# A gated attention and GLU kernel: raw gate and up pieces loaded seven steps ahead, the first round's transposed pieces in other buffers, output weight and last maxima fetched sooner, last sums later

## The chip, the core and the metric

The kernel runs on one core of a Trainium2 chip. The metric is the device time of one execution in microseconds (us), the median of several runs. The core has a matrix engine (PE, with its weight loads shown apart as PEld), a vector engine (DVE), a scalar engine (ACT), GpSimd (POOL), and SyncE (SP), which here does nothing but issue DMA transfers, one after the other in program order. All transfers of this kernel go through SP's one queue, and 16 DMA engines carry them out.

## The reference

The input x has 2048 tokens of 512 features. Two branches are computed from it and mixed with a gate of one number per token:

```python
g = sigmoid((x * gate_w).sum(-1, keepdims=True))
a = attention(x, wqkv, wo)     # 32 heads of 16, causal, window of 256 keys
b = (sigmoid(x @ w_gate) * (x @ w_up)) @ w_down     # hidden width 1376
return g * a + (1 - g) * b
```

All is float32. The kernel multiplies each pair of operands as high and low parts, with three matrix products (high by high, high by low, low by high).

## The kernel before, in words

**Two stretches.** The first stretch is a loop over `u` from 0 to `N - 1` (L764; `N` is 140). In it the attention is computed head group by head group: in step `u` scores by query block with their maxima (`s_part`, for `u` below 128), transposed scores with the exponential nine steps later (`st_part`), and, in every even step, the products with V of two blocks (`pv_part`, L807). Matrix products of the other branch fill the gaps: 72 groups of gate and up (`gu`, nine pieces of 128 hidden features, two matrices, four token chunks of 512), then 16 groups of the tail (`tp`, the last 224 hidden features, computed token block by token block). Results are stored to scratch tensors in DRAM: `gu_scratch`, `tail_scratch`, `oT_scratch` (attention output), `sum_scratch` (softmax sums).

The second stretch is a loop over `n` (L916), 44 steps of `(c, f)`: four rounds `c` of 512 tokens, with eleven pieces `f` of the hidden width each. Step `n` multiplies piece `f` with the down weight into four accumulators (`pd`, lines L79 to L81). At the end of a round the attention output is multiplied with the output weight (`pa`) and the two are mixed and stored.

**Raw pieces.** `h_load(n)` (L672) reads the gate and the up piece of step `n`, 512 KB, from `gu_scratch` into slot `n % 8` of `hv`, which lies over the buffer of V (16 blocks of 560 columns; a slot has 1024). Block by block V is read for the last time in the last steps of the first stretch, the last two blocks at `u` = 138. `h_skew(n)` (L708) prepares later steps: it splits the piece of step `n + 2` into high and low parts (`hb`: ACT L75, DVE L76) and computes sigmoid and product of step `n + 3` (ACT L727, DVE L728). `AHEAD` (L53) says how far ahead the pieces are loaded: `h_load(n + AHEAD)` in step `n` (L918), and the first `AHEAD` of them in the first stretch, every second `u` from `HLOAD = N - 2 * AHEAD` on (L858).

**Transposed pieces.** The pieces `f` = 9 and 10 come from the tail. `tail_read` (L696) reads them from `tail_scratch`, 14 transfers of 64 KB a round, transposed 32 by 32, to the place that `tail_home` (L679) gives: columns of `xh` and `xl` (the high and low parts of x) whose matrix work is done. For round 0 the transfers start at `u = TREAD` (L854), and what is left of them goes out in the first four steps of the second stretch (L921).

**Other transfers around the change.** `max_store` (L342) and `max_load` (L347) take the row maxima of four query blocks through DRAM into the operand `ring` that `st_part` reads; number 31, the last, holds query blocks 12 to 15 of the last group, and `st_part` needs the first of them at `u` = 131. `WO` (L793) loads the output weight, 1 MB, into the buffer that the gate and up weights leave. `sums_load`, `sums_invert` (L735, L739) read the softmax sums of a round, invert them on DVE (L741), and store them back (`rec_scratch`); round 3's are needed from the 34th step on. Transfers that wait for a result of the current step are put in the list `later` and issued with the next step (L781), and after the loop behind each of the last two tail groups (L868).

**What sets the order.** The program order on every engine is written out by hand (`manual_schedule`); an engine takes its instructions in that order, and SP too: a transfer whose wait isn't over holds all behind it.

Of the kernel before, what the change touches and what calls it, by code (L numbers as in the profile page):

```python
# [7 lines left out]
F32 = mybir.dt.float32  # L8
# [15 lines left out]
NC = T // CH  # L24
# [20 lines left out]
SHIFT = 6  # L45
TURN = ((0, 2, 1), (1, 0, 2))
TAIL = 109
TREAD = 136
WD_LOAD = {119: 0, 120: 1, 122: 2, 123: 3, 127: 4, 128: 5, 130: 6, 131: 7, 133: 8, 134: 9, 135: 10}
WO = 128  # L50
WO_SPLIT = {132: 0, 133: 1, 134: 2, 135: 3}
WD_SPLIT = {136: 8, 137: 9, 138: 10}
AHEAD = 5  # L53


@with_exitstack
def gated_mix_kernel(
# [46 lines left out]
    NSTEP = NG * NC  # L104
    NP = NSTEP // 2
    NU = NG * NB
# [3 lines left out]
    def load_d(f):  # L110
        tag = "draw" if f == 10 else "wqraw"
        raw_d[f] = cpool.tile([P, D], F32, tag=tag, name=f"wdraw{f}", bufs=2)
        nc.sync.dma_start(raw_d[f][0:FCH[f]], wd[f * P:f * P + FCH[f], :])
        if f == NF - 1:
            nc.sync.dma_start(raw_d[f][FCH[f]:], wd[f * P:f * P + QB, :])
# [13 lines left out]
    with ExitStack() as actx:  # L129
# [157 lines left out]
        def run_dmas(dmas):  # L287
            for dst, src in dmas:
                nc.sync.dma_start(dst, src)
# [54 lines left out]
        def max_load(s):  # L344
            st = ring[s // 2 % RING].bitcast(F32).rearrange("(a r) j f -> r a j f", r=QB)
            o = s % 2 * CH
            nc.sync.dma_start(  # L347
                st[0, :, 0:2, o:o + CH], max_d[s].rearrange("(p s) l b t -> (s l) p (b t)", p=2),
            )
# [31 lines left out]
        later = []  # L381
# [273 lines left out]
        def slot(h, d, c):  # L655
            return (xh, xl)[h][:, d, c * CH:(c + 1) * CH]
# [21 lines left out]

        def tail_home(c, f, w):  # L679
            k = 2 * (f - NFM) + w  # L680
            h, d, cc = (0, k, 2) if c % 2 == 0 else (1, k + 2, 2) if k < 2 else (0, k, 3)
            return (xh, xl)[h][:, d, cc * CH:(cc + 1) * CH].bitcast(F32)

# [12 lines left out]
        def tail_read(c, n):  # L696
            run_dmas(treads[c][:n])
            del treads[c][:n]
# [33 lines left out]
        def flat(v, c):  # L732
            return v[c].rearrange("h (q t) -> (h q) t", t=P)

        def sums_load(c):  # L735
            sm[c] = cpool.tile([P, P], F32, tag="sm", name=f"sm{c}", bufs=2)
            nc.sync.dma_start(sm[c], flat(sum_d, c))

        def sums_invert(c):  # L739
            t = sm.pop(c)  # L740
            nc.vector.reciprocal(t, t)  # L741
            return flat(rec_d, c), t
# [8 lines left out]
        N = NU + PVLAG + 1  # L751
        SUMS = NU - 13 + PVLAG + 1
        U_LAST = 4 * (NSTEP - 2 - 5)
        HLOAD = N - 2 * AHEAD
        done = 0
# [8 lines left out]
        for u in range(N):  # L764
            if u == LAG:
                vctx.close()
                ppool = actx.enter_context(tc.tile_pool(name="ppool", bufs=1))
                pv = ps.tile([P, CH], F32, tag="pv", name="pv", bufs=1)
                behind.append(lambda: nc.vector.memset(pv, 0.0))
            if u == 1:  # L770
                proj_post(NC)
            if u == 4:
                load_gu(0, 0)
                load_gu(0, 1)
            if u % 8 == 1 and u > 8 and u // 8 + 1 < NP:
                sdma = stack_build(u // 8 + 1)
            if u % 16 == 8 and u // 16 + 2 < NG:
                raw_q = load_wqk(u // 16 + 2)
            if u % 4 == 0 and 0 < u <= NU:
                max_store(u // 4 - 1)  # L780
            run_dmas(later)  # L781
            later.clear()
            run_dmas(sdma[:SD])
            del sdma[:SD]
            if u % 4 == 1 and 1 < u <= NU + 1:
                max_load(u // 4 - 1)
            if u in WD_LOAD:
                load_d(WD_LOAD[u])
            if u == TAIL:
                tail_room()  # L790
            if TAIL <= u < TAIL + 2 * ND and (u - TAIL) % 2 == 0:
                tail_load((u - TAIL) // 2)
            if u == WO:  # L793
                both = apool.tile([P, ND, CH], F32, tag="w0", name="woraw")
                wo_raw.extend(both[:, d] for d in range(ND))
                nc.sync.dma_start(both, wo.rearrange("(c p) n -> p c n", p=P))
            for s4 in proj_at.get(u, ()):
                if u < LAG:
                    first.insert(0, (
                        lambda k, h, s4=s4: proj_slot(s4, k, h), lambda s4=s4: proj_sum(s4)))  # L800
                else:
                    work.append(proj_group(s4))
            if u == NU + PVLAG - 1:
                hold_group(*rest.pop(0))
            for hh in range(HG):
                if hh == 0 and u % 2 == 0:
                    for w in (u - PVLAG - 1, u - PVLAG):  # L807
                        if 0 <= w < NU:
                            pv_part(w)
                if u < NU:  # L810
                    s_part(u, hh)
                if 0 <= u - LAG < NU:
                    st_part(u - LAG, hh ^ 1 if u < NU else hh)
                if u < LAG:
                    flush(behind)
                    if hh % 2 == 1:
                        upto = n_first * (2 * u + 1 + hh // 2) // (2 * LAG)
                        run_first(upto - done)
                        done = upto
                else:  # L820
                    if behind:
                        behind.pop(0)()
                    if acts and (u < NU or hh % 2 == 1):
                        acts.pop(0)()
                if u >= LAG and (hh < HG - 1 or u % 2 == 0 if u < NU else hh % 2 == 1):
                    next(slots, None)
                    if u >= NU and not (hh == HG - 1 and u % 2 == 1 and u > NU + 1):
                        next(slots, None)
            if u < LAG:
                flush(soon)  # L830
            if u == LAG - 1:
                split_gu(0, 0)
                split_gu(0, 1)
            if u % 4 == 3 and u < NU:
                max_split(u // 4)
            if u // 16 + 2 < NG:
                if u % 16 == 13:
                    acts.append(lambda g=u // 16 + 2, r=raw_q: (
                        split_wqk(g, r, 0), behind.append(lambda: split_wqk(g, r, 1))))
            if 0 <= u - LAG < NU:  # L840
                mask_p(u - LAG)
            if TAIL + 2 <= u <= TAIL + 2 * ND and (u - TAIL) % 2 == 0:
                acts.append(lambda d=(u - TAIL) // 2 - 1: tail_split(d))
            if WD_LOAD.get(u - 1, 8) < 8:
                acts.append(lambda f=WD_LOAD[u - 1]: split_d(f, True))
            if u in WO_SPLIT:
                acts.extend(lambda d=d: wo_split(d) for d in range(WO_SPLIT[u], WO_SPLIT[u] + 1))
            if u in WD_SPLIT:
                acts.append(lambda f=WD_SPLIT[u]: split_d(f, True))
            if SUMS <= u and (u - SUMS) % 4 == 0:  # L850
                sums_load((u - SUMS) // 4)
            if SUMS + 2 <= u and (u - SUMS) % 4 == 2:
                behind.append(lambda c=(u - SUMS) // 4: later.append(sums_invert(c)))
            if u == TREAD:  # L854
                tail_reads(0)
            if u >= TREAD:
                tail_read(0, 3)
            if u >= HLOAD and (u - HLOAD) % 2 == 0:  # L858
                h_load((u - HLOAD) // 2)
            if u >= N - 2:  # L860
                flush(acts)
                flush(behind)
                h_skew(u - N - 1)
        h_skew(-1)
        spare = [ppool.tile([P, 3, CH], F32, tag="pt", name=f"spare{k}", bufs=3) for k in range(3)]
        for group in rest:
            hold_group(*group)
            run_dmas(later)  # L868
            later.clear()
        assert not (work or first or going or behind or acts or raw_gu or sdma or pts or obs)  # L870

        def blocks(v):
# [13 lines left out]
        def gate():  # L886
            nc.scalar.activation(gs, gsum, AF.Sigmoid)
            nc.vector.tensor_scalar(omg, gs, -1.0, 1.0, op0=ALU.mult, op1=ALU.add)
# [27 lines left out]
        for n, (c, f) in enumerate(steps):  # L916
            if n + AHEAD < len(steps):
                h_load(n + AHEAD)  # L918
            h_skew(n)
# [11 lines left out]
                ]  # L931
            if n == 2:
                gate()
                last_sums = sums_invert(NC - 1)
            if n == 3:
                nc.sync.dma_start(*last_sums)
            if f < 8 and f % 2 == 0 and n > 0 or n == 1:
                o_load(4 * c + f // 2)
# [82 lines left out]
```

## Time and profile before

| what | us |
|---|---|
| median of 3 runs (lowest, highest) | 740.25 (738.74, 741.25) |
| the profiled execution, its own time | 739.3 |
| its span in the profile | 737.6 |
| first score maxima to last (`u` below 128), to about | 531 |
| rest of the first stretch, to about | 568.8 |
| round 0 of the second stretch, to about | 599.7 |
| round 1; round 2 | 40.9; 40.9 |
| round 3 with the last stores | 56.1 |

The chain of work that ended last runs over PE for 95% of the span, over DMA for 2% and over DVE for 2%. The largest groups of DMA transfers are 72 stores of 256 KB to `gu_scratch` and 36 loads of 512 KB from it.

How to read it: times in a timeline are us from the start of the span; a row gives start, length, engine, source line, operation, what it writes and reads, and in brackets the engine's idle time before it with what ended it. "SPq" is SP's queue: such a row is the issuing of a transfer, not the transfer. A matmul's row starts when PE starts it, and matmuls overlap, so the step from one start to the next is the pace. In the rows by stretch each engine has its busy us, then the number of its instructions; the last three columns are the granted clock of PE (1.00 is full), the mean busy share of the 16 DMA engines (their packets overlap a little, so it can pass 1) and GB/s.

### The profile page before, as it was taken

The numbers are of one execution on the slowest core, as the hardware profiler recorded it, in microseconds if no ns is written. First come the engines' busy times: TensorE is split into PE (matmuls) and PEld (weight loads), VectorE is DVE, ScalarE is ACT, GpSimd is POOL, SyncE is SP. The second block draws the span as 40 slices with busy tenths as digits, with TensorE's granted clock in tenths as the row PEclk, the third lists the DMA queues.
The fourth block names the chain that finished last, engine by engine and source line by source line (L and its number), as shares of the span: only waits on it lengthen the run. The fifth ranks groups of instructions, "written<-read, shape, count | busy, mean of one in ns | idle before, by whom it ended". The sixth has DMA issues, their size and how long they took to land.

```text
span 737.6 us, 17720 instructions
## 1 busy us (share of the span) xinstructions
PE 731.2 (99%) x6298; PEld 578.4 (78%) x6298; DVE 507.6 (69%) x1519; ACT 431.4 (58%) x922; POOL 170.6 (23%) x256
## 2 busy tenths in 40 slices
PE   9999999999999999999999999999999999999997
PEld 7888777887777878778777777777877778887886
DVE  5378867667776776776777677677846685848473
ACT  6423676576666666757657667675666573535341
POOL 5200333233232233323223322332341000000000
PEclk9999999999999999999999999999999999999999
DMA  8441334534435353452543525545287878879551
GB/s 295 111 116 44 101 103 123 154 82 131 131 113 142 89 149 113 124 150 68 156 114 103 152 72 138 157 128 152 68 261 215 231 196 201 194 182 228 143 133 57
DMA packets 94464, 103.65 MB, mean 141 GB/s; under 512 B 44942, under 2 KB 57486, under 8 KB 94376
## 3 DMA queue, kind: packets, MB, share of 16 engines
q1 hardware_dynamic: 94376, 102.53, 50.8%
q8 instruction: 49, 0.80, 0.5%
q14 instruction: 39, 0.32, 0.1%
HBM read 45.32 MB, written 31.99 MB: 105 GB/s over the span
## 4 chain that ended last, share of the span: by engine, by line
PE 95%; DMA 2%; DVE 2%; issue 1%; SPq 0%; ACT 0%; DVEq 0%; ACTq 0%
PE gu L245 28%; PE pv L394 12%; PE pj L245 11%; PE s L315 7%; PE st L361 5%; PE tp L539 5%; PE pd L81 4%; PE pd L79 4%; PE pd L80 4%; PE vh L576 3%; PE pa L79 2%; PE pa L81 2%; PE pa L80 2%; DMA V<-gu_scratch 1%; PE vps L440 1%; DVE junk L321 1%
## 5 line engine op out<-in xcount | busy, mean ns | idle before, releaser
L321 DVE CUSTOM_DVE_ANT_0 junk<-s,mask 128x384 f32<-128x384 f32 (+2 forms) x512 | 271.3, 530 | 123.6 <-PE s L315 56.2
L366 ACT ACTIVATE pt<-st 128x384 f32<-128x384 f32 (+2 forms) x512 | 240.9, 474 | 166.7 <-PE st L361 63.3
L245 PE MATMUL gu<-xh,w 64*128 64x512 f32 x1152 | 271.2, 393 | 0.0
L245 PE MATMUL gu<-xl,w 64*128 64x512 f32 x576 | 183.1, 392 | 0.0
L371 POOL TENSOR_SCALAR_AFFINE_SELECT pt<-pt 128x512 f32<-128x512 f32 x128 | 86.4, 675 | 373.7 <-ACT pt L366 370.1
L361 PE MATMUL st<-ring 64*128 64x384 f32 (+2 forms) x536 | 168.2, 332 | 0.1
L315 PE MATMUL s<-ring 64*128 64x384 f32 (+2 forms) x536 | 166.9, 329 | 0.7 <-DVE mx L321 0.7
L245 PEld LDWEIGHTS gu<-xh,w 64*128 64x128 f32 x1152 | 151.2, 185 | 13.6
L315 PEld LDWEIGHTS s<-ring 64*128 64x128 f32 x536 | 95.4, 184 | 39.9 <-DVE nm L332 8.1
L361 PEld LDWEIGHTS st<-ring 64*128 64x128 f32 x536 | 96.4, 184 | 10.5 <-issue 2.7
L394 PE MATMUL pv<-pt,V 128*32 128x384 f32 (+2 forms) x1408 | 91.0, 389 | 0.0
L245 PEld LDWEIGHTS gu<-xl,w 64*128 64x128 f32 x576 | 87.8, 185 | 3.9
L245 PE MATMUL pj<-xl,wqh 64*128 64x512 f32 (+1 forms) x228 | 80.1, 392 | 0.0
L245 PE MATMUL pj<-xh,wqh 64*128 64x512 f32 (+1 forms) x228 | 79.8, 392 | 0.0
L376 POOL TENSOR_SCALAR_AFFINE_SELECT pt<-pt 128x512 f32<-128x512 f32 x112 | 74.7, 667 | 0.0
L245 PE MATMUL pj<-xh,wql 64*128 64x512 f32 (+1 forms) x228 | 69.9, 391 | 0.0
L394 PEld LDWEIGHTS pv<-pt,V 128*32 128x32 f32 x1408 | 37.2, 109 | 35.0 <-issue 28.8
L79 PE MATMUL pd<-ring,hb 128*128 128x512 f32 x160 | 63.2, 395 | 0.3 <-ACT hb L75 0.3
L81 PE MATMUL pd<-ring,hb 128*128 128x512 f32 x160 | 63.1, 394 | 0.1
L80 PE MATMUL pd<-ring,hb 128*128 128x512 f32 x160 | 62.2, 389 | 0.0
L75 ACT CAST hb<-V 128x512 fp32r<-128x512 f32 x40 | 24.9, 622 | 52.5 <-DVE V L728 50.0
L245 PEld LDWEIGHTS pj<-xh,wql 64*128 64x128 f32 (+1 forms) x228 | 41.2, 185 | 3.1
(129 smaller groups left out, 1132.7 us busy)
## 6 DMA issues: line engine op xcount, KB each, us to landing
gu_scratch<-sp SPq DMA_DIRECT2D x72, 256.0 KB
V<-gu_scratch SPq DMA_DIRECT2D x36, 512.0 KB
ring<-sh SPq DMA_DIRECT2D x128, 128.0 KB
ring<-sl SPq DMA_DIRECT2D x64, 128.0 KB
guraw<-in_wgu_dram SPq DMA_DIRECT2D x18, 256.0 KB
oT_scratch<-ob SPq DMA_DIRECT2D x128, 32.0 KB
xl<-oT_scratch SPq DMA_DIRECT2D x16, 256.0 KB
out_dram<-spare SPq DMA_DIRECT2D x16, 256.0 KB
```

Source lines behind the costliest of these rows:

```text
L79: mm(ps, lh, rh, start=first, stop=False)
L80: mm(ps, lh, rl, start=False, stop=False)
L81: mm(ps, ll, rh, start=False, stop=last)
L245: mm(pt, (wl if w == 2 else wh)[r, d], (xl if w == 1 else xh)[r, d, c * CH:(c + 1) * CH], start=k == 0 and not second, stop=k == 3 * ND - ...
L315: mm(pt[:, (k - k0) * P:(e - k0) * P], lhsT, blk(g, k, hh, 1, e - k), start=k == k0, stop=e == i + 1, skip_group_check=True,)
L321: nc.vector.tensor_tensor_reduce(junk[:, 0:n], pt[:, 0:n], mask[:, 3 * P - n:], scale=1.0, scalar=NEG, op0=ALU.add, op1=ALU.max, accum_out ...
L361: mm(pt[:, (q - j) * P:(e - j) * P], lhsT, blk(g, q, hh, 0, e - q), start=q == j, stop=e == last, skip_group_check=True,)
L366: nc.scalar.activation(pts[u][:, hh, 0:n], pt[:, 0:n], AF.Exp, scale=SCALE)
L371: nc.gpsimd.affine_select(p[:, :, 0:P], p[:, :, 0:P], pattern=[[0, HG], [1, P]], compare_op=ALU.is_ge, fill=0.0, base=0, channel_multiplie ...
L376: nc.gpsimd.affine_select(p[:, :, 2 * P:], p[:, :, 2 * P:], pattern=[[0, HG], [-1, P]], compare_op=ALU.is_gt, fill=0.0, base=0, channel_mu ...
L394: mm(pv[32 * hh:32 * hh + 32, (q % 4) * P:(q % 4 + e - q) * P], V[:, j, h * VW:h * VW + 32], p[:, hh, (q - j) * P:(e - j) * P], start=Fals ...
L539: mm(tp[b][:, 0:TW], (xl if w == 1 else xh)[r, d, b * P:(b + 1) * P], tw[d][int(w == 2)][r, 0:TW], start=k == 0 and not second, stop=k == ...
```

## The change

Six edits:

- `AHEAD` from 5 to 7. Seven pieces are loaded in the first stretch, from `u` = 126 in place of 130, and in step `n` piece `n + 7`.
- The transposed pieces of round 0 go to columns 512 to 1023 of `xh` and `xl` for `d` 2 and 3, in place of columns 1024 to 1535 of `xh`. The tail groups read the new place in token blocks 4 to 7, the old one in 8 to 11.
- They are read from `u` = 133, two a step, in place of 136, three a step. Seven steps of two make all 14 in the first stretch; four steps of three left two.
- The output weight is loaded at `u` = 125 in place of 128.
- The last maxima are loaded at `u` = 128, right behind their store and one down weight, in place of 129.
- The sums of round 3 are loaded at step 3 of the second stretch, inverted at step 6 and stored at step 7, in place of the last `u`, step 2 and step 3. What the two last tail groups store goes out at step 3 as well.

```diff
-TREAD = 136
+TREAD = 133
-WO = 128
+WO = 125
-AHEAD = 5
+AHEAD = 7
...
         def tail_home(c, f, w):
             k = 2 * (f - NFM) + w
+            if c == 0:
+                return slot(k // 2, 2 + k % 2, 1).bitcast(F32)
...
-            if u % 4 == 1 and 1 < u <= NU + 1:
+            if u % 4 == 1 and 1 < u < NU:
                 max_load(u // 4 - 1)
             if u in WD_LOAD:
                 load_d(WD_LOAD[u])
+            if u == NU:
+                max_load(NSTEP - 1)
...
-            if SUMS <= u and (u - SUMS) % 4 == 0:
+            if SUMS <= u < N - 1 and (u - SUMS) % 4 == 0:
                 sums_load((u - SUMS) // 4)
...
             if u >= TREAD:
-                tail_read(0, 3)
+                tail_read(0, 2)
...
         for group in rest:
             hold_group(*group)
-            run_dmas(later)
-            later.clear()
...
             if n == 2:
                 gate()
+            if n == 3:
+                run_dmas(later)
+                sums_load(NC - 1)
+            if n == 6:
                 last_sums = sums_invert(NC - 1)
-            if n == 3:
+            if n == 7:
                 nc.sync.dma_start(*last_sums)
```

## The prediction

> **What bounds the kernel now.** I read the page first, then the rows by stretch, then the chain of waits, and last the timelines of SP and PE around the places that these named. The page:
>
> ```profile
> PE 731.2 (99%) x6298; PEld 578.4 (78%) x6298; DVE 507.6 (69%) x1519; ACT 431.4 (58%) x922; POOL 170.6 (23%) x256
> ```
>
> PE is busy for 731.2 of the span's 737.6 us, and the change neither adds nor takes a matmul. So all that it can move is PE's standing time, 6.4 us by this row, and small standstills between matmuls that the row still counts as busy. The rows by stretch say where the 6.4 us lie (time, then PE's busy us; the granted clock is 1.00 in all of them):
>
> ```profile
> 0.00:20.00 20.00, 18.47 (x78) 14.85 (x79) 9.88 (x16) 12.45 (x21) 12.04 (x14) 1.00 0.83 289
> ...
> 531.00:568.80 37.80, 37.69 (x370) 30.64 (x362) 19.97 (x44) 24.21 (x57) 12.60 (x18) 1.00 0.74 220
> 568.80:599.70 30.90, 30.59 (x133) 23.73 (x132) 23.84 (x45) 18.18 (x32) 0.00 (x0) 1.00 0.84 234
> 599.70:640.60 40.90, 40.90 (x185) 33.18 (x184) 27.48 (x49) 18.75 (x33) 0.00 (x0) 1.00 0.80 193
> ...
> 722.30:737.60 15.30, 11.56 (x53) 9.08 (x52) 3.69 (x5) 2.42 (x4) 0.00 (x0) 1.00 0.18 69
> ```
>
> The start (1.53 us) and the end (3.74 us) are out of the change's reach: it touches nothing before `u` = 125 and nothing behind step 34. In its reach lie 531 to 568.8 and round 0, with 0.11 and 0.31 us, and in round 1 PE never stands, though pieces are loaded only five steps ahead there too. The chain of waits names a transfer at one place of round 0 that matters:
>
> ```profile
> 576.15 5.06 DMA V<-gu_scratch
> ...
> 582.68 0.85 DVE sm L741
> ```
>
> A raw piece issued at 576.15 lands 5.06 us later; sigmoid, gate and the inversion of the last sums follow, and then PE. Here the change can gain, and it is small.
>
> **The change part by part. First, the raw pieces (AHEAD, and the sums with them).** SP's timeline shows why that piece, number 5, was late, and PE's what it cost:
>
> ```profile
> 573.23 0.33 SPq L737 DMA_DIRECT2D sm<-sum_scratch  x1
> 573.61 1.49 SPq L289 DMA_DIRECT2D xh<-tail_scratch  x3
> 575.20 0.91 SPq L289 DMA_DIRECT2D tail_scratch<-tt  x2
> 576.15 0.46 SPq L675 DMA_DIRECT2D V<-gu_scratch  x1
> ```
>
> ```profile
> 582.48 0.39 PE L80 MATMUL pd<-ring,hb 128*128 128x512 f32 x1
> 582.70 0.40 PE L81 MATMUL pd<-ring,hb 128*128 128x512 f32 x1
> 583.36 0.50 PE L79 MATMUL pd<-ring,hb 128*128 128x512 f32 x1 [0.26 <-ACT hb L75]
> 583.70 0.39 PE L80 MATMUL pd<-ring,hb 128*128 128x512 f32 x1
> 584.13 0.50 PE L81 MATMUL pd<-ring,hb 128*128 128x512 f32 x1
> 584.47 0.39 PE L79 MATMUL pd<-ring,hb 128*128 128x512 f32 x1
> ...
> 586.78 0.39 PE L80 MATMUL pd<-ring,hb 128*128 128x512 f32 x1
> 587.06 0.50 PE L81 MATMUL pd<-ring,hb 128*128 128x512 f32 x1
> 587.40 0.40 PE L79 MATMUL pd<-ring,hb 128*128 128x512 f32 x1
> ```
>
> Ahead of piece 5 on SP stand the load of the last sums, three transposed reads, and the stores of the last two tail groups, which wait for DVE. Matmuls of 512 columns start 0.22 to 0.23 us apart. From 582.70 to 584.47 there are four steps, 1.77 us in place of 4 x 0.23 = 0.92: **0.85 us** lost. At 587.06 the low part is again just in time: 0.62 us for two steps, **0.16 us** lost. The idle time in the row (0.26) shows less than a third of the first, since a late start also costs the matmuls behind it.
>
> After the change pieces 0 to 6 are issued in `u` = 126 to 138, each two steps behind the last reading of the V blocks that it overwrites (piece 0: blocks 0 and 1, read at 124; piece 6: blocks 10 to 12, read at 136), so SP doesn't stand for them. Piece 5 leaves at `u` = 136, where piece 3 left before:
>
> ```profile
> 560.79 0.49 SPq L675 DMA_DIRECT2D V<-gu_scratch  x1
> ```
>
> ```profile
> ACT V L727 <- DMA V<-gu_scratch: 21.0, 15, 4.0
> ```
>
> That is 15 us sooner than 576.15. Its sigmoid then follows ACT's chain instead of the transfer (the second row is ACT's waits for raw pieces, 15 in all; the longest, 4.0 us, is this one), so the split parts of step 5 are ready some 4 us sooner where 0.85 us were wanting. I take the whole 0.85 + 0.16 = 1.01 us as gained; least is 0, if another wait takes its place. The later rounds gain nothing by it: ACT's other waits there cost PE no time. What is late next shows in DVE's rows around step 0, with a transfer of SP's that will matter below:
>
> ```profile
> 558.17 0.37 SPq L737 DMA_DIRECT2D sm<-sum_scratch  x1
> ```
>
> ```profile
> 563.77 0.93 DVE L741 RECIPROCAL sm<-sm 128x128 f32<-128x128 f32 x1
> ...
> 567.41 0.69 DVE L728 TENSOR_TENSOR V<-V 128x512 f32<-128x512 f32 x1 [1.18 <-ACT V L727]
> ```
>
> DVE has two such instructions of 0.69 us a step for the pieces, product and low part, against PE's twelve matmuls of 0.23, 2.8 us: with the pieces there it draws ahead.
>
> The inversion of the last sums goes from step 2 to 6, one instruction of 0.93 us either way. Where it goes DVE is busy for 4.78 of 5.00 us:
>
> ```profile
> 590.00:595.00 5.00, 5.00 (x24) 4.10 (x23) 4.78 (x9) 4.51 (x9) 0.00 (x0) 1.00 0.62 177
> ```
>
> I cost it at nothing, covered by the lead of some 4 us; without that cover it is 0.93 us. In step `n` SP now waits for the slot of step `n - 1` in place of `n - 3`, whose reader (`h_skew(n - 3)`) is ahead of PE; the output loads queue behind it, and DVE needs those three steps later: nothing, unless SP falls behind.
>
> **Second, the last maxima and the output weight.** SP around `u` = 128, PE at `u` = 131, and PE's wait there:
>
> ```profile
> 534.27 0.43 SPq L796 DMA_DIRECT2D woraw<-in_wo_dram  x1
> ...
> 535.90 0.57 SPq L347 DMA_DIRECT2D ring<-max_scratch  x1
> ```
>
> ```profile
> 540.20 0.37 PE L539 MATMUL tp<-tail_hb,xh 64*128 64x450 f32 x1
> 540.41 0.39 PE L361 MATMUL st<-ring 64*128 64x384 f32 x2
> 540.59 0.36 PE L539 MATMUL tp<-tail_hb,xh 64*128 64x450 f32 x1
> ...
> 541.66 0.37 PE L539 MATMUL tp<-tail_wql,xh 64*128 64x450 f32 x1
> 542.14 0.45 PE L361 MATMUL st<-ring 64*128 64x384 f32 x2
> 542.38 0.36 PE L539 MATMUL tp<-tail_wqh,xh 64*128 64x450 f32 x1
> ```
>
> ```profile
> L361 PEldq EVENT_SEMAPHORE  x1: 51/51/51, 542.0 to 542.0; - x1
> ```
>
> The 16 KB of maxima leave at 535.90, behind the 1 MB of the output weight; PE's queue has a wait of its own at 542.0, in the first `st` that needs them, and goes on from there. That is 6.1 us for 16 KB. In the undisturbed round 540.20 to 540.59 takes 0.39 us, the disturbed one 541.66 to 542.38 takes 0.72: **0.33 us** lost. After the change the weight leaves in `u` = 125, behind the maxima before, where the queue is nearly empty:
>
> ```profile
> 523.00:530.00 7.00, 7.00 (x92) 6.11 (x82) 6.00 (x23) 3.90 (x9) 2.44 (x4) 1.00 0.19 57
> ```
>
> Its buffer is free: the last `gu` matmul starts at 509.17.
>
> ```profile
> 509.17 0.39 PE L245 MATMUL gu<-xh,w 64*128 64x512 f32 x1
> ```
>
> The maxima can leave no sooner than their store has landed, so at about the same time; SP stands there from 534.27 on, 1.6 us at most, with a raw piece and two tail stores behind it: the piece is needed in the second stretch, the stores' buffers four tail groups later. Only 256 KB is ahead of them now. I take 0.33 us as gained; least 0.
>
> **Third, the transposed reads.** 14 reads of 64 KB in 128-byte pieces, the same as before, two a step from `u` = 133 in place of three from 136. Their places are free when the tail groups 4 to 7 are done; the eighth of the 16 stores is the first here:
>
> ```profile
> 546.64 0.38 SPq L289 DMA_DIRECT2D tail_scratch<-tt  x1
> ```
>
> The price of one, from the packets of the 4.2 us from 561.8 on, in which five are issued:
>
> ```profile
> DMA packets 2429, 1.01 MB, mean 241 GB/s; under 512 B 2049, under 2 KB 2172, under 8 KB 2428
> ```
>
> 2049 small packets at 512 a read are four reads, so at most 4.2 / 4 = 1.05 us each. That matters for the third rival. I cost them at nothing: PE needs them in step 9 only. The tail stores put off to step 3 are read in round 3, so nothing again.
>
> **Sum:** 0.85 + 0.16 + 0.33 = 1.34 us less. Against the profiled execution's own 739.3: 738.0. That execution is 0.95 under the median of 740.25; taken off the median it is **738.9 us**. About 0.3% (2.2 us) is what a measurement of this kernel can tell from no change, so this lies within.
>
> **The rivals.** *More than the sum.* The three runs before lie 2.5 us apart, and both stalls hang on when a transfer lands; if a slower run is one in which they are longer, all runs after gather at the fast end. The fastest run less the sum: 738.74 - 1.34 = 737.4. For it: the maxima and piece 5 are the only late transfers behind which PE stood. Against it: the start, which waits for transfers too (DMA 0.83 busy), can vary as much.
>
> *Nothing.* Something else holds step 5: ACT and DVE come out of the first stretch with no lead (the product of step 0 starts only at 567.41), and DVE's two transposes of the last tail groups stay in the way. Then 740.25 less 0.33, 739.9. Against it: ACT's 4.0 us of standing for piece 5.
>
> *The crowd, slower.* From `u` = 132 to 135 four transposed reads go out with two raw pieces; before, it was two raw pieces alone. The loads of sums 2 and of the last down weights queue behind, the sums at 558.17. From 563.77 on DVE stands for late sums, with the low parts of the last weights and the product of step 0 behind it; the 1.18 us of idle time before that product cover the first of that. Four reads at 1.05 us make 4.2 us, less 1.18 is 3.0 us that step 0 starts later: 740.25 - 1.34 + 3.0 = 741.9. It decides when the sums land later than 564.95. For it: the maxima took 6.1 us behind 1 MB, more than the 5.6 from 558.17 to 563.77. Against it: the output weight is gone from the queue by then, and the price is an upper bound. [...]
>
> **How the numbers follow.** The forecast 0.54, within 0.3%. More than the sum 0.2: 737.4 is below 738.0, so faster. Nothing 0.1, the same. The crowd 0.16, of which 0.06 for a time over 742.5, with several such waits. A little of the forecast's own spread falls below 738.0: faster 0.22, same 0.72, slower 0.06. The range goes from 737.4 (the first rival) to 741.0, inside the crowd's 741.9, which leaves out less than 2 in 10.
>
> **What would show it.** In the changed kernel's trace: no step over 0.3 us between `pd` matmuls in steps 1 to 10; the `st` at `u` = 131 0.2 us behind the matmul before it; ACT L727 standing for raw pieces far less than 21.0 us; the reciprocal of sums 2 without idle time before it. Wrong would be a new wait of PE between 550 and 570, or a step 0 that starts later than 568.8.

## The result, and the profile after

| | before, us | after, us | ratio, 95% interval |
|---|---|---|---|
| median of 11 runs each on one chip (lowest, highest) | 740.9 (738.74, 743.55) | 737.95 (737.53, 738.54) | 0.9959 (0.9944 to 0.9974) |
| the profiled execution, its own time | 739.3 | 737.77 | |
| its span | 737.6 | 736.1 | |

The changed kernel is faster by 0.41%; the medians lie 2.95 us apart. (A ratio is worked out from all runs, so it can differ a little from the quotient of the medians.) The forecast of 738.9 was 0.95 us too high. The time lies between it and the 737.4 of the rival *more than the sum*, and what that rival says of the runs came: those after lie 1.0 us apart where those before lay 4.8. (One disturbed run of 1831.75 us of a kernel below is left out of its comparison.)

The page of the changed kernel, its span and busy times:

```profile
span 736.1 us, 17727 instructions
...
PE 730.0 (99%) x6298; PEld 578.3 (79%) x6298; DVE 507.1 (69%) x1519; ACT 430.4 (58%) x922; POOL 170.7 (23%) x256
```

PE stands for 6.1 us in place of 6.4, a difference of 0.3, though the span fell by 1.5: most of what a late start costs is counted as busy. So the starts have to be compared. Three matmuls of each profile, by the timelines of PE (the last `gu` of the first stretch of before, 509.17, and the first `pd`, 568.81, are known); the first `pa` matmul of round 0 in before:

```profile
600.08 0.50 PE L79 MATMUL pa<-xh 128*128 128x512 f32 x1
```

and the last `gu`, the first `pd` and the first `pa` in the changed kernel:

```profile
508.85 0.39 PE L245 MATMUL gu<-xh,w 64*128 64x512 f32 x1
...
568.19 0.48 PE L79 MATMUL pd<-ring,hb 128*128 128x512 f32 x1
...
598.39 0.50 PE L79 MATMUL pa<-xh 128*128 128x512 f32 x1
```

Up to 508.85 the gain is 0.32 us, which the change doesn't reach. From there to the first `pd` it is 59.64 - 59.34 = 0.30 us. Round 0, from the first `pd` to the first `pa`, takes 30.20 in place of 31.27: 1.07 us. The rest loses 0.2. PE's waits in the changed kernel hold only two groups, which before has with the same times, both ahead of the change's reach:

```profile
PE warm_ps L185 <- DVE warm L180: 1.2, 1, 1.2
PE s L315 <- DVE mx L321: 0.7, 2, 0.4
```

At `u` = 131 and in step 5, the two places of the prediction, PE now runs at its pace (timeline of PE in the changed kernel):

```profile
541.31 0.37 PE L539 MATMUL tp<-tail_hb,xh 64*128 64x450 f32 x1
541.36 0.37 PE L539 MATMUL tp<-tail_wql,xh 64*128 64x450 f32 x1
541.52 0.38 PE L361 MATMUL st<-ring 64*128 64x384 f32 x2
541.70 0.36 PE L539 MATMUL tp<-tail_wqh,xh 64*128 64x450 f32 x1
...
582.07 0.39 PE L81 MATMUL pd<-ring,hb 128*128 128x512 f32 x1
582.30 0.39 PE L79 MATMUL pd<-ring,hb 128*128 128x512 f32 x1
582.53 0.39 PE L80 MATMUL pd<-ring,hb 128*128 128x512 f32 x1
582.76 0.39 PE L81 MATMUL pd<-ring,hb 128*128 128x512 f32 x1
```

The `st` starts 0.16 us behind the matmul before it, and between steps 1 and 10 no `pd` start is more than 0.24 behind the last, but for one of 0.32 at the end of step 10, where before has 0.33. SP's order in the changed kernel (timeline of SP):

```profile
562.31 1.97 SPq L675 DMA_DIRECT2D V<-gu_scratch  x1
...
571.64 0.50 SPq L289 DMA_DIRECT2D sum_scratch<-ob  x1
572.50 0.90 SPq L289 DMA_DIRECT2D xl<-tail_scratch  x2
...
577.01 0.86 SPq L289 DMA_DIRECT2D tail_scratch<-tt  x2
578.29 0.32 SPq L739 DMA_DIRECT2D sm<-sum_scratch  x1
```

Piece 5 leaves at 562.31 in place of 576.15, and behind the store of the last sums (571.64) SP goes on 0.36 us after it is issued; the two tail stores and the load of the last sums follow later. In before SP stood there (its waits from 565 to 580 us: the load of the last sums waits for their store):

```profile
SPq L737 <- DMA sum_scratch<-ob: 1.4, 1, 1.4
```

ACT's list of waits has no raw piece any more (21.0 us before).

### The profile page after: what moved, and what is told of

It is laid out like the page before. It is cut to its first block, busy times and chain, and to the rows that moved or that the text cites. A ratio compares the mean times of both kernels' runs of the same rounds, so it can differ in the third digit from the quotient of the medians.

```text
span 736.1 us, 17727 instructions
## 1 busy us (share of the span) xinstructions
PE 730.0 (99%) x6298; PEld 578.3 (79%) x6298; DVE 507.1 (69%) x1519; ACT 430.4 (58%) x922; POOL 170.7 (23%) x256
## 4 chain that ended last, share of the span: by engine, by line
PE 97%; DVE 1%; DMA 1%; issue 1%; ACT 0%; SPq 0%; DVEq 0%
PE gu L245 28%; PE pv L394 12%; PE pj L245 11%; PE s L315 7%; PE st L361 5%; PE tp L539 5%; PE pd L79 5%; PE pd L81 5%; PE pd L80 5%; PE vh L576 3%; PE pa L79 2%; PE pa L80 2%; PE pa L81 2%; PE vps L440 1%; DVE junk L321 1%; DMA V<-in_wv_dram 1%
```

## The experiments

Two theories stood at first: **A**, that transfers which land late at varying times made the runs of before vary, and that AHEAD removes this; **B**, that something else varies. The results brought others in: **C**, the reads make the gain; **D**, the crowd of transfers from 560 to 586; **E**, a standstill of PE is followed by a lower clock; **F** and **G**, the last sums, their store and the last tail stores hold piece 5 up on SP; **H**, the inversion on DVE. Medians stand beside those of the kernel before, run in turn on the same chip.

**The kernel before again**, unchanged, one execution.

> The kernel before, unchanged, for a second profile beside its time. Its runs lie between 738.7 and 743.6 us, those of the changed kernel between 737.5 and 738.5. Theory A (the late transfers vary): where this run is slower than 739.3, the time over it stands in PE's rows at the `st` matmul of u = 131 and in the first steps of the second stretch, and the first 20 us are as before (PE busy 18.5 of 20). Theory B (something else varies, the start or the steady part): those two places lose 0.3 and 1.0 us again, and the excess lies elsewhere.

738.42 us, faster than 739.3, so this execution can't decide between A and B. Piece 5 was late as before (round 0 takes 31.22 us); at `u` = 131 PE's starts show 0.1 us lost (0.48 where 0.38 is the pace) in place of 0.33. So the loss at `u` = 131 varies from run to run, the one in step 5 was there again.

**AHEAD alone.**

```diff
-AHEAD = 5
+AHEAD = 7
```

> Only AHEAD from 5 to 7. Theory A: piece 5 leaves in the first stretch, step 5 of the second stretch has no standstill, profile about 1.0 us under 737.6, and most of the gain of the median too: 738.2 to 739.2, with runs closer together than before's 4.8 us. Theory B: 1.0 us less than before in the median (739.9), runs as far apart as before's. Theory C (the transposed reads' earlier start made the gain): no gain, 740 to 741, since twelve of the reads still go out from u = 136 on, now beside raw pieces.

740.28 (739.12 to 743.16, 12 runs) beside 740.03, ratio 1.0002 (0.9989 to 1.0015): nothing. Its profile, of an execution of 741.26, shows why (timelines of SP, DVE and PE):

```profile
575.03 0.33 SPq L737 DMA_DIRECT2D sm<-sum_scratch  x1
575.41 1.49 SPq L289 DMA_DIRECT2D xh<-tail_scratch  x3
577.00 0.91 SPq L289 DMA_DIRECT2D tail_scratch<-tt  x2
...
580.80 0.65 SPq L893 DMA_DIRECT2D xh<-rec_scratch  x1
...
586.83 0.01 DVE L900 LOAD_MASK_SELECT spare<-xh  x1 [5.25 <-DMA xh<-rec_scratch]
...
588.97 0.50 PE L81 MATMUL pd<-ring,hb 128*128 128x512 f32 x1 [1.71 <-DVE hb L76]
```

Pieces 5 and 6 had left at 561.74 and 568.79. But SP stood as before ahead of the load of the sums, and the reciprocal rows for the attention output (`rec_scratch`) left late behind it: DVE stood 5.25 us for them, and PE 1.71 for DVE. These rows were late in before too (timelines of SP and DVE in before):

```profile
578.96 0.65 SPq L893 DMA_DIRECT2D xh<-rec_scratch  x1
...
584.94 0.01 DVE L900 LOAD_MASK_SELECT spare<-xh  x1
```

They left 10.2 us behind the first `pd` there, 11.0 here, and 6.9 in the changed kernel (575.05). In before DVE, held by piece 5, came to them only at 584.94 and found them landed. So a second wait lay hidden behind the first, one step on and on another engine; moving piece 5 alone laid it open.

PE's waits in this kernel have another new line:

```profile
PE st L361 <- DMA ring<-max_scratch: 0.8, 1, 0.8
```

The weight left at 534.22, a raw piece at 534.75, the maxima at 536.49: with seven pieces one of them stands ahead of the maxima too. PE's wait at `u` = 131 is 0.8 us, and by the starts 1.1 us are lost (541.90 to 543.37 in place of 0.39).

**Maxima and weight alone.** `WO` 125, the last `max_load` at `u == NU`; nothing else.

```diff
-WO = 128
+WO = 125
```

> Only the output weight at u = 125 and the last maxima at u = 128. Theory A: the 0.33 us at u = 131 go, and more in slower runs, so 0.3 to 1.0 us less than before in the median; step 5 keeps its standstill. Theory B: 0.3 us less, which the runs can hardly tell. Theory C: no difference, within 0.3 us.

739.41 (738.38 to 743.74, 12 runs), ratio 0.9995 (0.998 to 1.0011). No loss at `u` = 131, and PE's 0.64 us of idle time in step 5 stays. The term is too small to be told from no change alone.

**The changed kernel with AHEAD 5.**

```diff
-AHEAD = 7
+AHEAD = 5
```

> The changed kernel with AHEAD back to 5, the other edits kept: the transposed reads from u = 133 in their new places, the last sums, maxima and weight as changed. Theory A: piece 5 leaves in step 0, but no longer behind transposed reads, sums and tail stores, so its standstill shrinks or goes; 738.0 to 739.5. Theory B: as the changed kernel but for the 1.0 us of step 5: 738.9. Theory C: the whole gain stays, 737.9 to 738.2.

737.69 (737.35 to 738.08, nine runs), ratio 0.9961 (0.9946 to 0.9976): as fast as the changed kernel. AHEAD is neither enough nor needed. A's attribution falls; its account of the varying stands.

**The reads alone**, sooner and in their new place.

```diff
-TREAD = 136
+TREAD = 133
-                tail_read(0, 3)
+                tail_read(0, 2)
+            if c == 0:
+                return slot(k // 2, 2 + k % 2, 1).bitcast(F32)
```

> Only the transposed reads: from u = 133, two a step, to the new places; five raw pieces ahead, sums, maxima and weight as before. Theory D (the crowd: from 560 to 586 us transposed reads, sums, tail stores, raw pieces and output loads share one queue, and what lands last stops ACT or DVE): the reads are the part that moves most work away, so most of the gain, 738.2 to 739.0, with at most the 0.3 us at u = 131 left over. Theory F (the last sums and the two tail stores ahead of piece 5 are what holds it): step 5 keeps its standstill, 739.5 to 740.2, as far apart as before.

739.23 (738.26 to 741.51, 12 runs) beside 739.65, ratio 0.9995 (0.9982 to 1.0009): nothing, so C falls, and D in so far as it put most of the gain on the reads. Piece 5 left at 577.07, with no reads of round 0 left to pass. PE stood longer than in before, and its clock stayed full (its timeline of PE, then its rows by stretch):

```profile
584.93 0.50 PE L79 MATMUL pd<-ring,hb 128*128 128x512 f32 x1 [2.08 <-ACT hb L75]
```

```profile
584.00:586.00 2.00, 1.02 (x3) 0.59 (x4) 2.00 (x5) 1.15 (x2) 0.00 (x0) 1.00 1.10 345
586.00:588.00 2.00, 2.00 (x10) 1.62 (x10) 1.97 (x5) 1.47 (x3) 0.00 (x0) 1.00 0.72 246
```

**The sums alone**, with the tail stores.

```diff
-            if SUMS <= u and (u - SUMS) % 4 == 0:
+            if SUMS <= u < N - 1 and (u - SUMS) % 4 == 0:
...
-            run_dmas(later)
-            later.clear()
...
+            if n == 3:
+                run_dmas(later)
+                sums_load(NC - 1)
+            if n == 6:
                 last_sums = sums_invert(NC - 1)
-            if n == 3:
+            if n == 7:
                 nc.sync.dma_start(*last_sums)
```

> Only the last sums and the stores of the last two tail groups put off to steps 3, 6 and 7. Theory D: piece 5 leaves a few us sooner but lands behind the same reads, a gain of 0 to 1 us, 739.0 to 740.0. Theory F: most of the gain, 738.0 to 738.6.

738.05 (737.5 to 738.38, 12 runs), ratio 0.9973 (0.9963 to 0.9984): nearly the whole gain, with AHEAD at 5. Its timelines of SP and ACT:

```profile
570.50 0.50 SPq L289 DMA_DIRECT2D sum_scratch<-ob  x1
571.33 1.44 SPq L289 DMA_DIRECT2D xh<-tail_scratch  x3
572.82 0.49 SPq L675 DMA_DIRECT2D V<-gu_scratch  x1
...
577.02 0.63 ACT L727 ACTIVATE V<-V 128x512 f32<-128x512 f32 x1 [0.28 <-DMA V<-gu_scratch]
```

Piece 5 leaves 3.3 us sooner than in before, and ACT stands 0.28 us for it in place of 4.04.

**Reads and sums together** (the two diffs above).

> Both of these edits, neither the seven pieces ahead nor the sooner maxima and weight. Theory D: no standstill of PE over 0.1 us between steps 1 and 10; the whole gain but for the wait at u = 131, 738.0 to 738.5. Theory F: the same as the sums alone.

737.85 (737.5 to 739.04, 12 runs), ratio 0.997 (0.9958 to 0.9981). The reads add nothing that can be measured.

**The kernel before with AHEAD 4**, to make the standstill longer.

```diff
-AHEAD = 5
+AHEAD = 4
```

> The kernel before with AHEAD = 4: piece 4 leaves in step 0, behind sums, reads and tail stores. Theory E (a standstill of some us in the second stretch lowers the granted clock for a while, which makes the slower runs of before: those over 741.3 show a mean clock of 0.997 in place of 1.0): PE stands 2 to 4 us at step 4, the granted clock drops behind it, mean 0.997, and the median is 741 to 744. Without theory E: the same standstill at a clock of 1.0, so only its own length, 740.5 to 742.5. If the number of pieces ahead doesn't matter as long as the crowd is there: as before, 740.

744.77 (744.75 to 748.41, 4 runs), ratio 1.0075 (1.0049 to 1.01). PE stood 2.32 us in step 4. Its rows by stretch, the last three columns clock, DMA and GB/s:

```profile
582.00:584.00 2.00, 1.46 (x5) 0.93 (x6) 1.16 (x2) 1.23 (x3) 0.00 (x0) 0.99 1.02 346
584.00:586.00 2.00, 2.00 (x7) 1.53 (x6) 1.77 (x5) 1.25 (x2) 0.00 (x0) 0.50 1.08 339
586.00:588.00 2.00, 2.00 (x8) 1.60 (x7) 1.97 (x5) 1.08 (x2) 0.00 (x0) 0.66 0.71 241
588.00:590.00 2.00, 2.00 (x10) 1.65 (x9) 1.82 (x4) 1.95 (x5) 0.00 (x0) 1.00 0.61 200
```

Behind the standstill PE got half the clock for (2 x 0.50 + 2 x 0.34) / 0.5 = 3.4 us, 1.7 us lost again. The standstill and the lower clock are what E expects; the median lies above its 741 to 744, since the later rounds lost time as well: in the profile round 1 is 0.55 us longer than in before, and round 3, with a second standstill of 0.96 us and matmuls that start 0.23 us apart again from 718.13 on, 1.6 us.

**Only the two tail stores later**, ahead of the store of the last inverted sums in step 3.

```diff
-            run_dmas(later)
-            later.clear()
...
             if n == 3:
+                run_dmas(later)
                 nc.sync.dma_start(*last_sums)
```

> The kernel before; only the stores of the last two tail groups are put off, to step 3. Theory G (what holds the queue is SP's order: SP stands for the sum store to land before it loads the last sums, then for DVE before the two tail stores, with piece 5 and all else behind): piece 5 leaves about 1 us sooner, a third of the gain, 739.0 to 739.5, runs still 2 to 4 us apart. Theory H (the inversion of the last sums in step 2 on DVE is what costs): no change, 739.6 to 740.2.

738.2 (737.7 to 739.34, 11 runs) beside 739.77, ratio 0.9974 (0.9963 to 0.9985). Its timeline of SP:

```profile
570.82 0.50 SPq L289 DMA_DIRECT2D sum_scratch<-ob  x1
573.66 0.33 SPq L737 DMA_DIRECT2D sm<-sum_scratch  x1
574.04 1.49 SPq L289 DMA_DIRECT2D xh<-tail_scratch  x3
575.57 0.49 SPq L675 DMA_DIRECT2D V<-gu_scratch  x1
```

SP stands from 571.32 to 573.66, between the store of the last sums and their load, which reads what that store writes. From the load to piece 5 it is 1.9 us, in before 2.9. So piece 5 leaves the 1 us sooner that G expects, counted from the load (0.6 us in time, as SP stood longer here), but the gain is far more than G's third of it.

**Only the last sums later**: loaded in step 3, inverted in 6, stored in 7; the tail stores stay.

```diff
-            if SUMS <= u and (u - SUMS) % 4 == 0:
+            if SUMS <= u < N - 1 and (u - SUMS) % 4 == 0:
...
+            if n == 3:
+                sums_load(NC - 1)
+            if n == 6:
                 last_sums = sums_invert(NC - 1)
-            if n == 3:
+            if n == 7:
```

> The kernel before; only the last sums are put off (load in step 3, inversion in step 6, store in step 7), the tail stores stay where they were. Theory G: SP no longer stands about 2 us for the sum store, piece 5 leaves about 2 us sooner, most of the gain, 738.1 to 738.8. Theory H: the same gain, since the inversion moves too.

738.14 (737.61 to 738.74, 9 runs), ratio 0.9974 (0.9964 to 0.9983). Its timelines of SP and ACT:

```profile
570.88 0.50 SPq L289 DMA_DIRECT2D sum_scratch<-ob  x1
571.64 1.54 SPq L289 DMA_DIRECT2D xh<-tail_scratch  x3
573.28 0.91 SPq L289 DMA_DIRECT2D tail_scratch<-tt  x2
574.24 0.46 SPq L675 DMA_DIRECT2D V<-gu_scratch  x1
...
578.61 0.63 ACT L727 ACTIVATE V<-V 128x512 f32<-128x512 f32 x1 [1.53 <-DMA V<-gu_scratch]
```

Without the load the stand is 0.26 us (571.38 to 571.64), and piece 5 leaves 1.9 us sooner than in before. Either half alone gives nearly the whole gain: F and G hold, and what decides is a margin.

**Only the inversion later**, the load in its old place.

```diff
+            if n == 6:
                 last_sums = sums_invert(NC - 1)
-            if n == 3:
+            if n == 7:
                 nc.sync.dma_start(*last_sums)
```

> The kernel before; only the inversion of the last sums goes to step 6 and its store to step 7, the load stays in the last step of the first stretch. Theory G: piece 5 leaves as late as before, ACT stands for it as long; at most 0.3 us gained of the 0.9 us that DVE spends on the inversion, 739.2 to 740. Theory H: nearly the whole gain, 738.0 to 738.6.

739.84 (738.99 to 742.03, 11 runs), ratio 1.0001 (0.9989 to 1.0013): nothing, so H falls. The profile caught an execution of 741.65 us, which shows what such a one is made of (its timeline of PE, then its rows by stretch):

```profile
584.35 0.50 PE L79 MATMUL pd<-ring,hb 128*128 128x512 f32 x1 [1.66 <-ACT hb L75]
```

```profile
584.00:586.00 2.00, 1.65 (x6) 1.08 (x7) 1.44 (x4) 0.93 (x2) 0.00 (x0) 0.97 1.09 342
586.00:588.00 2.00, 2.00 (x6) 1.53 (x5) 1.97 (x4) 1.61 (x3) 0.00 (x0) 0.50 0.87 284
588.00:590.00 2.00, 2.00 (x8) 1.57 (x7) 1.67 (x3) 1.93 (x5) 0.00 (x0) 0.68 0.62 181
590.00:592.00 2.00, 2.00 (x10) 1.67 (x9) 1.97 (x5) 1.76 (x3) 0.00 (x0) 1.00 0.72 238
```

A standstill of 1.66 us, and again about 3.4 us at half clock behind it.

**The changed kernel with sums and tail stores in their old places** (the sums' diff above, undone in it).

> The changed kernel with the last sums and tail stores as before: the other five edits without the one that alone gave the gain. Theory G: piece 5 leaves in time, but SP still stands in the same place, and the next transfers behind it, the rows and the output for step 3, are late in place of it, as in the run with AHEAD alone, though nearer to time since the reads are gone: 738.3 to 739.5. If the other edits suffice by themselves too: 737.7 to 738.2.

739.09 (737.76 to 741.23, 11 runs), ratio 0.9988 (0.9976 to 1.0): most of the gain is lost. As with AHEAD alone, DVE stood 4.93 us for the `rec_scratch` rows, issued at 579.36, and PE 1.38 us for DVE.

**Round 0 in the kernels with five pieces ahead.** Issue of piece 5; start of its sigmoid behind the first `pd`; round 0 from the first `pd` to the first `pa`, by the timelines of each profile:

| kernel | piece 5 issued | sigmoid behind step 0 | round 0, us |
|---|---|---|---|
| sums alone | 572.82 | 8.66 | 30.19 |
| reads and sums | 573.89 | 9.51 | 30.19 |
| only the sums later | 574.24 | 9.90 | 30.21 |
| changed, AHEAD 5 | 574.11 | 10.26 | 30.23 |
| only the tail stores later | 575.57 | 11.92 | 30.56 |
| before | 576.15 | 12.43 | 31.27 |
| before again | 575.08 | 12.54 | 31.22 |
| maxima and weight alone | 576.02 | 12.80 | 31.50 |
| only the inversion later | 576.67 | 13.81 | 34.01 (clock down to 0.50) |
| reads alone | 577.07 | 14.24 | 32.88 |

By an estimate from these rows (12.43 less the 1.07 us lost there, 14.24 less 2.68) a late piece costs nothing up to about 11.5 us; from there each us costs about one. The changed kernel itself, without a wait for piece 5, takes 30.20. So the margin is small: with the tail stores out of the way, 1 us less ahead of piece 5, 0.36 us of round 0's loss of 1.07 are left.

## Why the prediction was right on the two losses, and wrong on what removes them and on the size

**The two losses: right.** Profile against profile the sum holds term by term: 1.07 us in round 0 where 1.01 was forecast, 0.30 between the last `gu` and the first `pd` where 0.33 was.

**What bounds: right.** PE, with its standing time all that can move. No version here beats the changed kernel beyond its spread: AHEAD 5 gives 737.69, reads and sums 737.85, the changed kernel 737.95, the sums alone 738.05.

**Taking the sum off the median: wrong, and this is the step that failed for the time.** "That execution is 0.95 under the median of 740.25; taken off the median it is 738.9 us": that takes every run's losses to be the profiled run's. The 87 runs of the kernel before that stood beside the experiments say otherwise. In 68 of them the mean clock was 0.999 or 1.0, and they took 739.6 us on average (738.35 to 741.26). In 19 it was 0.997 or 0.998, and they took 741.9 (741.2 to 743.23). The 68 lie 1.6 us above the 738.0 that the 11 runs of the changed kernel average, 0.25 more than the 1.34; what these 0.25 are stays open. The 19 add 19/87 x 2.3 = 0.5 on the average of all. Averages thus lie 1.6 + 0.5 = 2.1 us apart. The 2.95 of the first comparison is more because four of its 11 runs of before lie above 742, where 8 of the 87 do. None of the 19 has a profile. What they are made of is argued from the execution of 741.65 us above, of a kernel in which only the inversion comes later: the standstill longer, then half clock. In the 64 compared runs of the six kernels in which piece 5 leaves before 576 and the sums or tail stores are later, the mean clock is never below 0.999.

In these profiles the length of a standstill alone doesn't tell whether half clock follows. Standstills of 1.66 us (only the inversion later) and of 2.32 us (AHEAD 4) were followed by about 3.4 us of it, while one of 2.08 us (reads alone) and one of 1.71 (AHEAD alone) were not: the clock stayed at 1.00 there. In both cases with half clock it began 1.4 to 1.5 us behind the end of the standstill (at about 585.88 and 583.96 by the rows above). What decides between them stays open.

**"AHEAD, and the sums with them": the attribution was wrong.** The prediction named what stood ahead of piece 5 on SP and then credited the gain to moving the piece away from there. It took "the whole 0.85 + 0.16 = 1.01 us as gained; least is 0, if another wait takes its place". With AHEAD alone another wait did, at PE's cost of 1.71 us in that profile. The step that failed is "the output loads queue behind it, and DVE needs those three steps later: nothing, unless SP falls behind." SP was behind, but not for a slot of the pieces: the last sums and tail stores still stood ahead of the rows. What gained was to take these away, the load that waits for a store just issued (SP's stand of 1.9 us in before) or the issuing of the two stores (0.95 us). The prediction has the two stores wait for DVE; in before they are issued 0.1 us behind the reads (573.61 + 1.49 to 575.20), with DVE's last transpose for them done by 573.22, so they cost their issuing and no wait. That the whole change still gained is in part luck: it holds the edit that works, which was costed at nothing, beside the one that was credited.

**The inversion at nothing: right.** Moving it alone did nothing (1.0001), and the round of the changed kernel is free of standstills.

**Maxima and weight: right within its bounds of 0 to 0.33, and a varying term.** Of the profiles with the old order the loss was 0.1 us in before again and absent with the sums alone and in others; with AHEAD alone it grew to 1.1. Whether the weight's move is what keeps it at none in the changed kernel, with seven pieces, wasn't tried.

**The crowd: didn't come.** The load of sums 2 left at 559.23, behind four reads issued from 549.76 on, and DVE's inversion of them follows without idle time (timeline of DVE in the changed kernel):

```profile
562.52 0.65 DVE L545 STREAM_TRANSPOSE tt<-tp 128x448 f32<-128x448 f32 x1 [0.49 <-PE tp L539]
563.10 0.12 DVE L546 COPY gsum<-tp 128x1 f32<-128x1 f32 x1
563.14 0.93 DVE L743 RECIPROCAL sm<-sm 128x128 f32<-128x128 f32 x1
```

Step 0 starts at 568.19, no later than 568.8. The 741.9 had counted the four reads as all outstanding when the sums leave; the last of them was issued by 553.8, 5.5 us ahead. No run here shows the sums waiting behind the reads: the reads alone, sooner, cost nothing (0.9995).

**"Nothing": didn't come**, though ACT and DVE do enter with no lead: the first `pd` matmuls, from 568.19 on, are still 0.32, 0.39 and 0.34 us apart.

## What to carry to other kernels

When a transfer is late, look at what the issuing engine stood for ahead of it: moving the late transfer forward can lay open the wait for the next one, which is late for the same reason; taking away what stands ahead (a load of what was stored just before, stores that nobody needs yet) helps all of them. Read a standstill from the starts of the matmuls, not from the idle time; and before a sum is taken off a median, look at how far the runs lie apart and at their mean clock, since the runs at the slower end may hold the same loss in a larger size.

## What the runs showed of the hardware

Standstills of 1.66 us (only the inversion later) and 2.32 us (AHEAD 4) in an otherwise full PE were followed, 1.4 to 1.5 us after their end, by about 3.4 us at a granted clock of 0.50, 1.7 us of work lost; those of 0.96 (AHEAD 4, round 3), 1.38 (sums and tail stores in their old places), 1.71 (AHEAD alone) and 2.08 us (reads alone) were not. A load that reads what a store has just been told to write held SP for 1.5 to 2.3 us (AHEAD 4; only the tail stores later), and everything behind it.
